# Indexed filling of free page rows and a reordered start, in a fused attention and mixture-of-experts kernel

## The chip, the cores and the metric

The kernel runs on one core of a Trainium2 chip. The metric is device time in microseconds (us) of one execution. The core has a matrix engine (TensorE, PE), a vector engine (VectorE, DVE), a scalar engine (ScalarE, ACT), a general engine (GpSimd, POOL) and SyncE (SP), which here only issues transfers. Each engine works through its own list of instructions in order and waits on semaphores for the others. Transfers run on 16 shared DMA engines.

## The reference

Block-causal attention over 8 batches of 8 heads, 576 tokens and width 64, followed by a mixture of 8 experts in which each of the 4608 tokens goes to its best expert:

```python
scores = scale * np.matmul(q, k.transpose(0, 1, 3, 2))
mask = block_i >= block_j            # blocks of 64
attn = softmax(np.where(mask, scores, -1e9))
x = (attn @ v) -> (4608, 512)        # all heads of a token side by side

logits = x @ w_gate
expert_idx = np.argmax(logits, axis=1)
gate_w = softmax(logits)[arange(N), expert_idx]
for e in range(8):
    rows = tokens with expert_idx == e
    y[rows] = np.maximum(x[rows] @ w1[e], 0) @ w2[e]
return gate_w[:, None] * y
```

## The kernel before

**Two stages.** The attention stage handles 32 head pairs (`PAIRS`), four to a batch. The expert stage handles pages of 128 token rows, each page belonging to one expert. Between them lies `xsorted`, a buffer in device memory with 43 pages (`NP` = 36 + 7). A row has 258 words (`ROW`): 512 half-precision values of x, the gate weight, and the number of the token.

**A head pair.** `load` (L171) fetches q and k of a pair from SP's queue, `load_v` (L185) its v. `cast` (L195) turns q and k to half precision on POOL: two instructions on L199 and one for the tail of 64 tokens on L201. `trans` (L204) transposes them on PE and copies the result out on DVE (L215, L217). `scores` (L225) multiplies, takes the exponential on ACT (L245) and zeroes masked corners on POOL (L247). `sums` (L249) adds tiles on DVE for the denominators; `attend` (L258) multiplies by v (L273); `denominators` (L279) uses the constant `picks`; `finish` (L301) multiplies by `wgi`, which holds an identity and the gate weights side by side (L320), and by `sel` (L316), and divides on DVE. The tiles for q and k and for v have two buffers each, so the load of a pair three ahead waits for a cast, and that of v for an attend.

**A batch.** After its fourth pair `choose` picks each token's expert. Four or five pairs later `route` (L384 to L436) counts tokens by expert and gives each token a slot in `xsorted`; `cnt`, `pages`, `lastA` and `used` carry the state: tokens and pages of each expert so far, where its last page lies, and pages in use. `scatter` (L442) then writes rows to their slots with an indexed DMA from POOL, five to a batch. `load_weights` (L138, L142) fetches the experts' weights in 16 parts of 1 MB, also from POOL's queue.

**Fills.** A page that ends up partly used would hold old data in its free rows. So `fill_pages` (L122) writes rows whose token number is `NO_TOKEN` over pages before tokens arrive: in pairs 0 to 3, eight DMAs from SP cover all 43 pages. Later the rows with `NO_TOKEN` are dropped on output, since the indexed store checks its bounds.

**An expert page.** `step(T)` issues, for PE: the first matmul of page T (`m1`, L626), the transposes of page T+1 (`mtx`, L611), the transposes of the hidden layer of page T-1 (`mth`, L638) and the second matmul of page T-2 (`m2`, L648). ACT computes h of page T (L631) and then y of page T-2 (L651), in this order. POOL stores y by token number (L652). There are two h tiles and two y tiles. `mload` (L602) loads a page five steps ahead from SP; ten page tiles exist. In step 1 the last batch is routed and scattered. `closed`, `first_places` and `orders` pick ten pages that no later token can touch (`FIRST`), so these can start early; their loads do not wait for the last batch's rows.

**Branches.** 36 pages are always processed. Behind them, nested branches on `used` process up to 38, up to 40, or all 43; `ends` holds these counts. 38 pages are processed with the data of the runs shown: the store L652 stands 38 times in the profile.

**Order.** PE, ACT and POOL follow the order written in the main loop during attention (`manual_schedule`, L523); in the expert stage only PE and ACT do (L699). DVE and SP throughout, and POOL in the expert stage, are ordered by the scheduler.

**Start.** Before the first load is used, L51 to L119 and L159 to L167 set up all constants on POOL: identities, triangles, `picks`, `wgi`, `sel`, counters, the `fill` row and borders of tiles.

Of the kernel before, what the change touches and what calls it, by code (L numbers as in the profile page):

```python
# [8 lines left out]
F32 = mybir.dt.float32  # L9
F16 = mybir.dt.float16  # L10
I32 = mybir.dt.int32
# [11 lines left out]
def kernel(  # L23
# [28 lines left out]
    make_identity(nc, ident32)  # L52
    ident16 = consts.tile([128, 128], F16)
    nc.gpsimd.tensor_copy(ident16, ident32)
    before32 = consts.tile([128, 128], F32)
    make_upper_triangular(nc, before32, 1.0, diag=False)
    before16 = consts.tile([128, 128], F16)
    nc.gpsimd.tensor_copy(before16, before32)
    ones16 = consts.tile([128, 128], F16)
    nc.gpsimd.memset(ones16, 1.0)  # L60

    picks = consts.tile([128, 5, 32], F32)
    nc.gpsimd.memset(picks, 0.0)
    for i in range(5):
        nc.gpsimd.memset(picks[:, i, i:i + 1], 1.0)

    wgi = consts.tile([128, HP, 144], F32)
    nc.gpsimd.memset(wgi, 0.0)
    for hp in range(HP):
        nc.gpsimd.tensor_copy(wgi[:, hp, 0:128], ident32)  # L70
        for h in range(2):
            nc.sync.dma_start(
                out=wgi[h * 64:h * 64 + 64, hp, 128 + h * E:128 + h * E + E],
                in_=moe_w_gate[hp * 128 + h * 64:hp * 128 + h * 64 + 64, :])

    GROUP = (0, 1, 0, 1, 0)
    sel = consts.tile([128, 5, 2], F32)
    for i in range(5):
        for h in range(2):
            r = 32 * (2 * h + GROUP[i]) + i  # L80
            nc.gpsimd.tensor_copy(sel[:, i, h:h + 1], ident32[:, r:r + 1])
    ione = consts.tile([128, E], F32)
    nc.gpsimd.memset(ione, 1.0)
    pref_i = consts.tile([128, 5, E], I32)
    nc.gpsimd.iota(pref_i, pattern=[[0, 5], [-1, E]], base=E, channel_multiplier=0)
    pref = consts.tile([128, 5, E], F32)
    nc.gpsimd.tensor_copy(pref, pref_i)
    page_i = consts.tile([128, 1], I32)
    nc.gpsimd.iota(page_i, pattern=[[0, 1]], base=0, channel_multiplier=1)
    page_f = consts.tile([128, 1], F32)  # L90
    nc.gpsimd.tensor_copy(page_f, page_i)
    em_all = consts.tile([128, B], F32)

    FIRST = 10
    order1 = consts.tile([1, 2 * FIRST], I32)
    order2 = consts.tile([1, 2 * (NP - FIRST)], I32)
    place_i = consts.tile([128, NP], I32)
    nc.gpsimd.iota(place_i, pattern=[[1, NP]], base=0, channel_multiplier=0)
    place = consts.tile([128, NP], F32)
    nc.gpsimd.tensor_copy(place, place_i)  # L100
    page_h = consts.tile([128, 1], F16)
    nc.gpsimd.tensor_copy(page_h, page_f)
    nc.gpsimd.memset(em_all, 0.0)
    used_i = consts.tile([1, 1], I32)
    cnt = consts.tile([128, E], F32)
    pages = consts.tile([128, E], F32)
    lastA = consts.tile([128, E], F32)
    used = consts.tile([128, 1], F32)
    for t in (cnt, pages, lastA, used):
        nc.gpsimd.memset(t, 0.0)  # L110


    wall = wpool.tile([128, E, 16, 512], F16)


    fill = consts.tile([128, ROW], I32)
    nc.gpsimd.memset(fill, 0)
    nc.gpsimd.iota(fill[:, 257:258], pattern=[[0, 1]], base=NO_TOKEN,
                   channel_multiplier=0)  # L119
    xs_pages = xsorted.rearrange("(t p) r -> p t r", p=128)  # L120

    def fill_pages(b):  # L122

        def upto(n):
            return min(NP, -(-n * S // 128) + E - 1) if n else 0
        lo, hi = upto(b), upto(b + 1)
        if hi > lo:
            nc.sync.dma_start(out=xs_pages[:, lo:hi, :],
                              in_=fill.unsqueeze(1).to_broadcast([128, hi - lo, ROW]))

    def apart(key, ins):
        tc.declare_no_dep(ins.ins, group=key, reason="scatters to different rows")
# [13 lines left out]
    with tc.tile_pool(name="ld", bufs=2) as ld, \  # L146
# [9 lines left out]
        ptp = probs.enter_context(tc.tile_pool(name="ptp", bufs=2))  # L156

        oTs = [op.tile([128, 640], F32, name=f"oT{i}") for i in range(2)]
        for t in oTs:  # L159
            nc.gpsimd.memset(t[:, 576:640], 0.0)  # L160
        dens = [op.tile([128, 128], F32, name=f"den{i}") for i in range(2)]

        acc = op.tile([128, 2, 512], F32)
        nc.gpsimd.memset(acc[:, :, 448:512], 1.0)
        ohs = [op.tile([128, 5, E], F16, name=f"oh{i}") for i in range(2)]
        for t in ohs:
            nc.gpsimd.memset(t, 0.0)  # L167

        st, yps = {}, []

        def load(p):  # L171
            b, h0 = p // HP, 2 * (p % HP)

            qk = ld.tile([128, 2, 2, 256], F32, name="qk32")
            tl = ld.tile([64, 2, 2, 64], F32, name="tl32")
            for n, src in ((0, q), (1, k)):
                nc.sync.dma_start(
                    out=qk[:, n],
                    in_=src[b, h0:h0 + 2, 0:512, :].rearrange("h (p c) d -> p h (c d)", c=4))
                nc.sync.dma_start(  # L180
                    out=tl[:, n],
                    in_=src[b, h0:h0 + 2, 512:576, :].rearrange("h p d -> p h d"))
            st["qk", p] = (qk, tl)
# [11 lines left out]
        def cast(p):  # L195
            qk, tl = st.pop(("qk", p))
            h16 = op.tile([128, 2, 5, 2, 64], F16, name="qk16")
            for n in range(2):
                nc.gpsimd.tensor_copy(h16[:, n, 0:4].rearrange("p c h d -> p h c d"),  # L199
                                      qk[:, n].rearrange("p h (c d) -> p h c d", c=4))  # L200
            nc.gpsimd.tensor_copy(h16[0:64, :, 4], tl)  # L201
            st["qk16", p] = h16
# [143 lines left out]
        def small(name, w=E):  # L346
            return rp.tile([128, w], F32, name=name)
# [90 lines left out]
        def scatter(b, j):  # L438
# [8 lines left out]
            if b == B - 1:  # L447
                tc.add_to_no_dep_group("last rows", ins.ins)

        def closed():  # L450

            cur, hit = small("cur"), small("hit")
# [56 lines left out]
        def last_experts():  # L509
            st["em_h"] = experts()  # L510
# [12 lines left out]
        with tc.manual_schedule(engines={ET.PE, ET.Activation, ET.Pool}):  # L523
# [9 lines left out]
            for n in range(2):  # L533
                trans(1, n)
            load(2)
            for p in range(PAIRS):
                nxt, more = p + 1 < PAIRS, p + 2 < PAIRS
                if nxt:
                    load_v(p + 1)
                if p + 3 < PAIRS:  # L540
                    load(p + 3)
                for b in ((0,), (1, 2), (3, 4), (5, 6, 7), ())[min(p, 4)]:
                    fill_pages(b)
                if more:
                    cast(p + 2)
                sums(p)
                if nxt:
                    scores(p + 1, 0)
# [106 lines left out]
                in_=y, in_offset=None, bounds_check=N - 1, oob_is_err=False)  # L655
            apart("tokens", ins)

        ends = list(range(-(-N // 128), NP, 2))[:3] + [NP]

        def step(T, n):  # L660
            if T < n:
                m1(T)
            if T == 1:
                route(B - 1)
                for j in range(5):
                    scatter(B - 1, j)
                last_experts()
            if T == 3:
                last_order()
            if T + 5 < ends[0]:  # L670
                mload(T + 5)
            if T == ends[0] - 2:
                for t in range(ends[0], NP):
                    mload(t)
            if T + 1 < n:
                mtx(T + 1)
            if 0 <= T - 1 < n:
                mth(T - 1)
            if 0 <= T - 2 < n:
                m2(T - 2)  # L680
# [58 lines left out]
```

## Time and profile before

| | us |
|---|---|
| median of 3 runs | 470.23 |
| lowest, highest | 461.27, 476.65 |
| the profiled execution | 470.48 |
| its span, first to last instruction | 468.7 |
| its mean granted PE clock | 0.97 |

The page gives, for each engine, the time in which it was busy and its number of instructions; then groups of instructions by line, with the number, the busy time, the mean of one in ns, and behind the second bar the time that the engine stood idle just before them and what ended it. A waiting time `3.73 <-DMA v<-in_v_dram` in a timeline row means that the engine stood idle so long until that transfer had landed. SPq and POOLq rows are the issuing of transfers. The attention stage lies between about 8 and 286 us, the expert stage after it. The transfers that the change touches stand on the page as follows (KB each, and the median us from issue to landing where it is known):

```
xsorted<-x,slot POOLq DMA_INDIRECT x40, 4.1
out_dram<-y,xs POOLq DMA_INDIRECT x38, 2.7
xsorted<-fill SPq DMA_DIRECT2D x4, 516.0 KB
xsorted<-fill SPq DMA_DIRECT2D x3, 645.0 KB
xsorted<-fill SPq DMA_DIRECT2D x1, 1548.0 KB
```

The transfers that fetch q and k are of 256 KB each and 32 KB for the tails; those of v are of 128 and 16 KB, two of each to a pair; a part of the weights has 1024 KB at its destination.

### The profile page before, as it was taken

The numbers are of one execution on the slowest core, as the hardware profiler recorded it, in microseconds if no ns is written. First come the engines' busy times: TensorE is split into PE (matmuls) and PEld (weight loads), VectorE is DVE, ScalarE is ACT, GpSimd is POOL, SyncE is SP. The second block draws the span as 40 slices with busy tenths as digits, with TensorE's granted clock in tenths as the row PEclk, the third lists the DMA queues.
The fourth block names the chain that finished last, engine by engine and source line by source line (L and its number), as shares of the span: only waits on it lengthen the run. The fifth ranks groups of instructions, "written<-read, shape, count | busy, mean of one in ns | idle before, by whom it ended". The sixth has DMA issues, their size and how long they took to land.

```text
span 468.7 us, 11177 instructions
## 1 busy us (share of the span) xinstructions
PE 420.8 (90%) x3870; PEld 260.5 (56%) x3870; DVE 252.2 (54%) x755; ACT 196.6 (42%) x309; POOL 191.3 (41%) x378
## 2 busy tenths in 40 slices
PE   2899879897999999999988897999999999999880
PEld 1466656575666666566656574555555555555430
DVE  2476946894696987977875954422222222222210
ACT  1455435444445454555453431334344343443420
POOL 8263335556347566566274440241222212222120
PEclk9999989999999999999999988899999999999986
DMA  5599979878869988989788478032222223222211
GB/s 138 141 278 242 233 192 230 194 194 200 164 180 208 219 202 187 212 210 190 190 201 206 89 151 197 24 125 96 101 93 85 86 91 103 102 88 75 92 49 43
DMA packets 85195, 71.46 MB, mean 152 GB/s; under 512 B 52240, under 2 KB 79632, under 8 KB 83088
## 3 DMA queue, kind: packets, MB, share of 16 engines
q1 hardware_dynamic: 78000, 39.71, 32.6%
q0 software_dynamic: 7136, 30.98, 27.7%
q8 instruction: 36, 0.59, 0.6%
q14 instruction: 23, 0.19, 0.1%
HBM read 67.56 MB, written 20.40 MB: 188 GB/s over the span
## 4 chain that ended last, share of the span: by engine, by line
issue 24%; DMA 11%; POOL 7%; PE 6%; DVE 4%; SPq 2%; POOLq 1%; DVEq 0%
POOL out_dram L652 7%; DMA v<-in_v_dram 5%; DMA out_dram<-y,xs 5%; PE o L273 3%; DMA xs<-xsorted 2%; PE tp L320 1%; PE tp L296 1%; POOL xsorted L442 1%; DVE qkT L215 1%; SPq L602 1%; DVE acc L251 1%; PE s L242 1%; SPq L192 0%; POOLq L652 0%; DVE acc L253 0%
## 5 line engine op out<-in xcount | busy, mean ns | idle before, releaser
L245 ACT ACTIVATE pt<-s 128x1024 f32<-128x1024 f32 x96 | 94.7, 1022 | 84.9 <-PE s L242 68.0
L273 PE MATMUL o<-pt,v 128*64 128x320 f32 (+3 forms) x768 | 97.1, 397 | 8.1 <-DMA v<-in_v_dram 8.1
L652 POOL DMA_INDIRECT out_dram<-y,xs x38 | 37.4, 984 | 114.2 <-ACT y L651 113.6
L626 PE MATMUL s<-wall,xsT 128*128 x304 | 75.7, 394 | 6.4 <-issue 3.1
L273 PEld LDWEIGHTS o<-pt,v 128*64 128x64 f32 x768 | 56.5, 142 | 44.1 <-issue 12.4
L215 DVE COPY qkT<-tp 128x512 f16<-128x512 f16 x64 | 43.7, 683 | 52.1 <-PE tp L213 52.1
L648 PE MATMUL tp<-wall,hT 128*128 x304 | 71.7, 379 | 0.0
L614 DVE COPY xsT<-o 128x512 f16<-128x512 f16 x38 | 16.1, 424 | 100.5 <-PE o L611 100.5
L247 POOL MEMSET pt<- 64x128 f32 x128 | 23.2, 200 | 97.5 <-ACT pt L245 86.4
L631 ACT ACTIVATE h<-s 128x1024 f16<-128x1024 f32 x38 | 38.9, 1023 | 53.7 <-PE s L626 53.7
L442 POOL DMA_INDIRECT xsorted<-x,slot x40 | 47.4, 1185 | 32.7 <-DVE em_h L471 20.1
L199 POOL CAST qk<-qk 128x512 f16<-128x512 f32 x64 | 50.9, 818 | 19.3 <-DMA qk<-in_q_dram 9.7
L320 PE MATMUL tp<-wgi,oT 128*128 128x144 f32 x320 | 56.0, 309 | 0.0
L626 PEld LDWEIGHTS <-xsT 128*128 128x128 f16 x304 | 30.4, 100 | 44.0 <-issue 7.9
L651 ACT ACTIVATE y<-tp,xs 128x512 f32<-128x512 f32 x38 | 26.1, 687 | 53.7 <-PE tp L648 50.9
L277 ACT COPY oT<-o 128x256 f32<-128x256 f32 x64 | 25.7, 402 | 50.0 <-PE o L273 50.0
L320 PEld LDWEIGHTS tp<-wgi,oT 128*128 128x128 f32 x320 | 43.7, 194 | 3.0 <-issue 0.2
L648 PEld LDWEIGHTS <-hT 128*128 128x128 f16 x304 | 28.4, 98 | 27.2
L251 DVE TENSOR_TENSOR acc<-pt 128x896 f32<-128x896 f32 x32 | 36.3, 1135 | 13.1 <-issue 7.6
L242 PE MATMUL s<-qkT 64*128 64x512 f16 (+4 forms) x320 | 33.7, 302 | 2.5 <-DVE qkT L215 1.8
L211 PE MATMUL tp<-ident,qk 128*128 128x128 f16 x256 | 26.3, 227 | 7.8 <-POOL qk L199 7.8
L641 DVE COPY hT<-o 128x1024 f16<-128x1024 f16 x38 | 26.3, 691 | 12.2 <-PE o L638 9.7
(137 smaller groups left out, 481.9 us busy)
## 6 DMA issues: line engine op xcount, KB each, us to landing
wall<-in_moe_w_dram POOLq DMA_DIRECT2D x16, 1024.0 KB, 9.4
qk<-in_q_dram SPq DMA_DIRECT2D x32, 256.0 KB
qk<-in_k_dram SPq DMA_DIRECT2D x32, 256.0 KB
v<-in_v_dram SPq DMA_DIRECT2D x64, 128.0 KB
xs<-xsorted SPq DMA_DIRECT2D x43, 129.0 KB
xsorted<-fill SPq DMA_DIRECT2D x4, 516.0 KB
xsorted<-fill SPq DMA_DIRECT2D x3, 645.0 KB
xsorted<-fill SPq DMA_DIRECT2D x1, 1548.0 KB
```

The lines of the kernel that those rows point to most:

```text
L199: nc.gpsimd.tensor_copy(h16[:, n, 0:4].rearrange("p c h d -> p h c d"), qk[:, n].rearrange("p h (c d) -> p h c d", c=4))
L215: nc.vector.tensor_copy(qkT[:, n, 0:512].rearrange("d (p c) -> d p c", c=4), ps[:, 0:512].rearrange("d (c p) -> d p c", c=4))
L242: nc.tensor.matmul(out=sp[:, h, o:o + w], lhsT=qkT[r, 1, c * 128:c * 128 + 128], rhs=qkT[r, 0, q0:q0 + w], start=True, stop=True)
L245: nc.scalar.activation(pt[:, :, t * 512:t * 512 + 512], sp, AF.Exp, scale=scale)
L251: nc.vector.tensor_tensor(out=acc[:, :, 0:448], in0=pt[:, :, 128:576], in1=pt[:, :, 576:1024], op=ALU.add)
L273: nc.tensor.matmul(out=o[h * 64:h * 64 + 64, q0 - lo:hi - lo], lhsT=vt[r, c, h, :], rhs=src, start=(c == 0), stop=(c == last), skip_group_ ...
L320: nc.tensor.matmul(out=ps[:, m * 144:m * 144 + 144], lhsT=oT[:, i * 128:i * 128 + 128], rhs=wgi[:, hp, :], start=True, stop=True, skip_gro ...
L442: ins = nc.gpsimd.indirect_dma_start(out=xsorted[:, :], out_offset=bass.IndirectOffsetOnAxis(ap=slot[0:m, j:j + 1], axis=0), in_=x16[0:m, ...
L626: nc.tensor.matmul(out=hp[:, half * 512:half * 512 + 512], lhsT=xT[:, c * 128:c * 128 + 128], rhs=weight(T, 2 * c + half), start=(c == 0), ...
L631: nc.scalar.activation(h, hp, AF.Relu)
L648: nc.tensor.matmul(out=yp, lhsT=hT[:, f * 128:f * 128 + 128], rhs=weight(T, 8 + f), start=(f == 0), stop=(f == 7))
L652: ins = nc.gpsimd.indirect_dma_start(out=out[:, :], out_offset=bass.IndirectOffsetOnAxis(ap=xs[:, 257:258], axis=0), in_=y, in_offset=None ...
```

## The change

Five things are edited.

1. The fills of pairs 0 to 3 go. One fill of the pages from 36 on stays, placed at pair 4 in the loop. The other free rows are computed once the last batch is routed (`free_rows`, six small DVE instructions) and written by eight indexed DMAs from POOL, one for each expert, two in each of the steps 2 to 5 (`fill_rows`). An index that is not a free row is out of bounds and is dropped.
2. k of pairs 0 and 1 is loaded from ACT's queue instead of SP's.
3. k of pairs 0 and 1 is cast on DVE instead of POOL.
4. Constants are set up later: some after the first scores (`borders`, `constants`, then the loads in `gate_weights`), those that only routing uses in pair 1 (`route_constants`). Only the identity stays ahead of the first cast.
5. `ends` has one more level: 36, 38, 40, 42, 43 instead of 36, 38, 40, 43.

```diff
+    row_m = consts.tile([128, 1], F32)
+    row_n = consts.tile([128, 1], F32)
...
+    def gate_weights():
+        for hp in range(HP):
+            for h in range(2):
+                nc.sync.dma_start(
+                    out=wgi[h * 64:h * 64 + 64, hp, 128 + h * E:128 + h * E + E],
+                    in_=moe_w_gate[hp * 128 + h * 64:hp * 128 + h * 64 + 64, :])
+
+    def constants():
+        nc.gpsimd.memset(fill, 0)
+        nc.gpsimd.iota(fill[:, 257:258], pattern=[[0, 1]], base=NO_TOKEN,
+                       channel_multiplier=0)
+
+        nc.gpsimd.memset(picks, 0.0)
...
+        nc.gpsimd.memset(wgi, 0.0)
+        for hp in range(HP):
+            nc.gpsimd.tensor_copy(wgi[:, hp, 0:128], ident32)
...
+    def route_constants():
+        make_upper_triangular(nc, before32, 1.0, diag=False)
...
+        nc.gpsimd.tensor_scalar(row_m, page_f, -128.0, None, op0=ALU.add)
+        nc.gpsimd.tensor_scalar(row_n, page_f, -float(NO_TOKEN), None, op0=ALU.add)
...
+        def borders():
+            nc.gpsimd.memset(acc[:, :, 448:512], 1.0)
+            for t in oTs:
+                nc.gpsimd.memset(t[:, 576:640], 0.0)
+            for t in ohs:
+                nc.gpsimd.memset(t, 0.0)
...
             for n, src in ((0, q), (1, k)):
-                nc.sync.dma_start(
+                eng = nc.scalar if n and p < 2 else nc.sync
+                eng.dma_start(
...
             for n in range(2):
-                nc.gpsimd.tensor_copy(h16[:, n, 0:4].rearrange("p c h d -> p h c d"),
+                eng = nc.vector if n and p < 2 else nc.gpsimd
+                eng.tensor_copy(h16[:, n, 0:4].rearrange("p c h d -> p h c d"),
...
+        def free_rows():
+
+            got, w = small("got"), small("frw")
+            nc.vector.scalar_tensor_tensor(out=got, in0=pages, scalar=-128.0, in1=cnt,
+                                           op0=ALU.mult, op1=ALU.add)
+            nc.vector.tensor_scalar(got, got, row_m, None, op0=ALU.is_le)
+            nc.vector.scalar_tensor_tensor(out=w, in0=lastA, scalar=-1.0, in1=pages,
+                                           op0=ALU.add, op1=ALU.add)
+            nc.vector.tensor_scalar(w, w, 128.0, row_n, op0=ALU.mult, op1=ALU.add)
+            nc.vector.tensor_tensor(out=w, in0=w, in1=got, op=ALU.mult)
+            rows = rp.tile([128, E], I32, name="frows")
+            nc.vector.tensor_scalar(rows, w, float(NO_TOKEN), None, op0=ALU.add)
+            st["free"] = rows
+
+        def fill_pages():
+
+            nc.sync.dma_start(out=xs_pages[:, N // 128:, :],
+                              in_=fill.unsqueeze(1).to_broadcast([128, NP - N // 128, ROW]))
+
+        def fill_rows(n):
+            ins = nc.gpsimd.indirect_dma_start(
+                out=xsorted[:, :],
+                out_offset=bass.IndirectOffsetOnAxis(ap=st["free"][:, n:n + 1], axis=0),
+                in_=fill, in_offset=None, bounds_check=NP * 128 - 1, oob_is_err=False)
+            apart("rows", ins)
+            tc.add_to_no_dep_group("last rows", ins.ins)
...
             load(2)
+            borders()
+            constants()
+            gate_weights()
             for p in range(PAIRS):
...
-                for b in ((0,), (1, 2), (3, 4), (5, 6, 7), ())[min(p, 4)]:
-                    fill_pages(b)
                 if more:
                     cast(p + 2)
+                if p == 1:
+                    route_constants()
+                if p == 4:
+                    fill_pages()
...
-        ends = list(range(-(-N // 128), NP, 2))[:3] + [NP]
+        ends = list(range(-(-N // 128), NP, 2)) + [NP]
...
                 for j in range(5):
                     scatter(B - 1, j)
+                free_rows()
                 last_experts()
+            if 2 <= T < 6:
+                for e in range((T - 2) * E // 4, (T - 1) * E // 4):
+                    fill_rows(e)
```

## The prediction

> **What bounds the kernel now.** I read the page first (busy shares, costliest groups), then the waits of TensorE (PE), then the timeline at the places where it waits.
>
> ```profile
> PE 420.8 (90%) x3870; PEld 260.5 (56%) x3870; DVE 252.2 (54%) x755; ACT 196.6 (42%) x309; POOL 191.3 (41%) x378
> L273 PE MATMUL o<-pt,v 128*64 128x320 f32 (+3 forms) x768 | 97.1, 397 | 8.1 <-DMA v<-in_v_dram 8.1
> ```
>
> PE is the bound in both stages, so a change is worth what it does to PE's gaps. The row L316 comes once a head pair; its starts are 7.71 us apart where nothing waits (24.66, 32.37, 40.08, 47.80) and 8.62 where a batch is routed. In the expert stage the page rhythm is 4.18 us. Three places matter here. The start:
>
> ```profile
> 7.14 1.16 POOL L199 CAST qk<-qk 128x512 f16<-128x512 f32 x2
> 7.79 0.61 PE L211 MATMUL tp<-ident,qk 128*128 128x128 f16 x4 [7.79 <-POOL qk L199]
> 10.41 1.03 PE L242 MATMUL s<-qkT 64*128 64x512 f16 x6 [0.79 <-DVE qkT L215]
> ```
>
> POOL is busy without a break from 0.75 to 7.14 us with constants, and only then casts q and k one after the other; PE waits 7.79 us for it. Next, 56 to 70 us:
>
> ```profile
> 46.94 3.10 SPq L128 DMA_DIRECT2D xsorted<-fill  x3
> 50.15 1.33 SPq L189 DMA_DIRECT2D v<-in_v_dram  x1
> 54.60 3.60 SPq L192 DMA_DIRECT2D v<-in_v_dram  x1
> 57.47 0.61 PE L242 MATMUL s<-qkT 64*128 64x512 f16 x6
> 61.81 4.48 PE L273 MATMUL o<-pt,v 128*64 128x256 f32 x24 [3.73 <-DMA v<-in_v_dram]
> 60.00:68.00 8.00, 6.05 (x48) 4.20 (x49) 1.80 (x8) 1.06 (x3) 2.95 (x6) 0.79 0.63 166
> ```
>
> Three fills (13 pages of 129 KB, 1.68 MB) are issued just ahead of v; issuing itself slows to 3.60 us for one load; the DMA engines are full (share 1.05 in 52 to 60 us); PE waits 3.73 us for v. The 24 matmuls that follow take 4.48 us against 2.81 us elsewhere, and the granted clock of that window is 0.79 (the column after POOL). The interval of L316 is 13.37 us (56.42 to 69.79): 5.65 above 7.72. Two later v waits, of 2.2 and 2.1 us, have no fill near them (intervals of 12.19 and 10.45 us, together 7.2 above rhythm). Last, the early expert stage:
>
> ```profile
> 306.41 0.90 POOL L442 DMA_INDIRECT xsorted<-x,slot  x1 [0.30 <-issue]
> 307.62 1.00 POOL L652 DMA_INDIRECT out_dram<-y,xs  x1 [0.30 <-issue]
> 308.92 0.99 POOL L652 DMA_INDIRECT out_dram<-y,xs  x1 [0.30 <-issue]
> 314.70 0.69 ACT L651 ACTIVATE y<-tp,xs 128x512 f32<-128x512 f32 x1 [1.42 <-PE tp L648]
> 316.43 1.02 ACT L631 ACTIVATE h<-s 128x1024 f16<-128x1024 f32 x1 [1.05 <-PE s L626]
> 320.57 0.66 PE L638 MATMUL o<-ident,h 128*128 128x128 f16 x8
> ```
>
> Five scatters of the last batch go out from 301.34 at about 1.27 us each; the first output rows, ready at 302.56, already wait for them until 307.62. After two outputs POOL has caught up.
>
> [...] a wait of 3.73 us was followed by 1.67 us of slowness, one of 2.2 us by about 2.3, so I add 1.9 us to each wait of that size. [...] The trace cannot show two issuing queues; it shows 229, 190 and 165 GB/s in the third, fourth and fifth microsecond. [...]
>
> **Part by part.** In the order of the built program:
>
> *First loads and casts.* k of pairs 0 and 1 is issued by ACT and cast by DVE; POOL makes only the identity (0.75 to 1.4 us) before its cast of q. The bytes decide: 576 KB (q, k and their tails of pair 0) had moved by about 4.9 us (23, 229, 190 and most of 165 KB in microseconds 1 to 5). With two queues interleaved, q and k come together at about 4.5 to 4.9, plus an estimated 0.7 until the semaphore is seen, judged from the 1.1 us between the first issue (0.76) and the first bytes (1.9). Cast of q 0.62, identity to f16 0.28: first transposes at 6.3 (5.7 to 6.9) instead of 7.79. The tail's cast (0.39) follows, while DVE has cast k beside it; before, k's cast and the tail put the second transposes at 8.85, now about 7.0. So scores start 1.9 us earlier; I take **2.0** (1 to 3[...]). ACT's four issues (about 0.6 each) and its table load (1.28) end at 4.6, before its first exponential. VectorE's room instruction, once first in its queue, moves behind pair 1.
>
> *Constants moved.* After pair 0's four memsets, which end at 14.33 us in the trace and so at about 12.3 then, POOL does borders, fill, picks, the gate tile and sel: 0.19+0.22+0.19+0.42+0.45+1.54+1.24 = 4.3 us, to about 16.6; the cast of pair 2 (1.8 us) ends at 18.4, and its transposes (21.54 in the trace) are due at 19.5. Hidden with 1 us to spare. The eight gate loads sit behind four pairs' loads and the one remaining fill in SP's queue, and wait for the gate memset: issued about 14 to 19 us (8 x 0.6), landed by 21; their first reader L320 is due at about 22. Zero, at most 1.5. The second group of constants (about 20 small instructions, 3.0 us by their rows) follows pair 3's cast at about 24 us and holds the memsets of pair 2, which are not needed before 31, and VectorE's room, queued ahead of pair 3's transposes' copies, due at 27.5. Zero, at most 1.
>
> *Fills dropped.* Eight fills of 43 pages, 5.68 MB, become one of 7 pages, 0.92 MB, which stands early in SP's queue, before the gate loads. 4.76 MB leave the queue. Up to 48 us PE waited for none of it: no gain. At 50 to 62 us v no longer has 1.68 MB ahead of it: **-5.6**. The floor is 0, if the weight load issued at 47.31 on POOL's queue holds v back instead; the ceiling is -12.8, if the two later v waits (7.2) go too, which no fill explains. SP's order of v against q also shifts by a few places later on; its price is unknown, I take 0 (-3 to +3).
>
> *Fills by index.* Six VectorE instructions of 128x8 (0.15 us each) at page 1 delay the next page's copy by 0.6 us; PE is in 1.89 us of matmuls then. Zero. Eight indirect DMAs, priced as the indexed stores they resemble (0.98 + 0.30 = 1.28 us), come on POOL's queue in this order: five scatters, two fills, output 0, six fills, output 1, output 2. Output 0 goes from 307.62 to 310.2; output 1 from 308.92 to 301.34 + 5 x 1.26 + 9 x 1.28 = 319.2. There are two y tiles, so y of page 3 (due 314.70) waits until output 1 has landed: 319.2 + 2.7 (median of the DMA issues) = 321.9. Behind it on ACT is h of page 6 (due 316.43): it ends at 321.9 + 0.7 + 1.0 = 323.6, and PE's transposes of h, due 320.57, wait **3.0 us**; with 1.9 of half clock **+4.9**. If most indices, being out of range, make a fill cost half (0.64), output 1 is 5.1 earlier and nothing waits: floor 0. If the landing counts from the end of POOL's work and a fill takes 1.5, the wait is 6: ceiling +8. Page 10's load now waits for the last fill too (about 321); it is read at about 332: zero.
>
> *The extra branch level.* Both programs leave at 38 pages by the same branches: zero.
>
> Sum: -2.0 - 5.6 + 4.9 = **-2.7 us** against the profiled execution's 470.5 (its span 468.7 and 1.8 around it), which stands 0.25 above the median of 470.23: 467.5, rounded to **467**.
>
> **The rivals.** *A, POOL's jam costs nothing*: for it, POOL is 0.13 to 0.24 busy later in the stage and the fills mostly skip rows; against it, output 0 already waited 5 us behind five scatters. 463 us. *B, the later v waits go as well* (DMA share falls, loads gain a lead): for it, the runs of before spread by 15 us, as such waits would; against, loads are held to two buffers, so no lead survives 60 us. 467 - 7 = 460. *C, slower*: the v wait at 58 us belongs to the 1 MB weight load and not to the fills; it would stay, leaving -2.0 + 4.9 = +2.9, so 473. It decides if v of pair 5 lands after 58.1 us (its attend's turn), less the 2 us of the earlier start. For it: the two later waits stand beside weight loads alone; against: other pairs with a weight load run at 7.71. To be slower by over 2% (9.4 us) it would need a jam at its ceiling (+8) too and a little more. That the fills are not dropped is excluded: the built queue of SP has one.
>
> **How the numbers follow.** Likeliest case 0.47, A 0.15, B 0.18, C 0.15, C with the long jam 0.05. A change of 2% is about what a measurement of this kernel can tell from none. Faster by that (below 461) takes B and half of what A and B share: 0.20. Slower by it (above 480) takes the last case and some of C's upper end: 0.08. The rest, 0.72, is within 2%. The range, from B's 460 less its spread to C's 473 plus the spread of the runs shown, is 458 to 475.
>
> **What would show it.** First L211 on PE near 6.3 us and first L242 near 8.5. No PE wait for v between 50 and 70 us, an L316 interval of 7.7 to 8.6 there, DMA share below 0.9. POOL rows of two fills, one output, six fills; then one ACT wait for an output of about 7 us, PE's L638 late by about 3 us and half clock after it. The forecast is wrong if v still waits at 56 us, if fills take under 0.9 us each, or if L320 or the copies of pair 3 wait for constants.

## The result, and the profile after

The changed kernel takes **475.81 us** (median of 4 runs, 474.19 to 478.99), the kernel before 465.75 us (4 runs, 461.04 to 476.65): a ratio of **1.033, 95% interval 1.022 to 1.043**. It is slower, and outside the range of 458 to 475. (Two of the four runs of the kernel before, and its profiled execution, were slow runs; medians here are of all runs, ratios of the fast ones alone, which makes the ratio larger than the 1.022 of the medians.) The profiled execution took 474.19 us, its span is 472.4 us.

Line numbers have moved: L276 is the old L273 (attention), L661 the old L626 (first expert product), L673 the old L638 (transposes of h), L683 the old L648 (second product), L687 the old L652 (output). L473 is the indexed fill.

From the page: busy shares, and two of the costliest groups.

```profile
PE 417.0 (88%) x3870; PEld 256.9 (54%) x3870; DVE 253.9 (54%) x763; ACT 196.3 (42%) x309; POOL 201.9 (43%) x386
...
L661 PE MATMUL s<-wall,xsT 128*128 x304 | 76.7, 398 | 20.2 <-DVE xsT L649 12.0
L276 PE MATMUL o<-pt,v 128*64 128x320 f32 (+3 forms) x768 | 93.0, 389 | 0.6 <-DMA v<-in_v_dram 0.6
```

The columns of the groups are number, busy time, mean of one in ns, and idle time just before them with what ended it. The 8.1 us of waits for v have gone to 0.6. In their place the first expert product waits 20.2 us. The start, from the timeline of the changed kernel:

```profile
4.64 0.54 DVE L202 CAST qk<-qk 128x512 f16<-128x512 f32 x1 [4.64 <-DMA qk<-in_k_dram]
4.85 0.48 POOL L54 CAST ident<-ident 128x128 f16<-128x128 f32 x1
...
5.39 0.59 PE L214 MATMUL tp<-ident,qk 128*128 128x128 f16 x4 [5.39 <-POOL ident L54]
...
7.63 1.03 PE L245 MATMUL s<-qkT 64*128 64x512 f16 x6 [0.79 <-DVE qkT L218]
```

The first scores come at 7.63 us, not 10.41. The stretch in which v was late, by windows of 8 us (the columns are PE, PEld, DVE, ACT, POOL, granted clock, DMA share, GB/s):

```profile
52.00:60.00 8.00, 7.49 (x90) 5.13 (x90) 7.78 (x38) 3.75 (x8) 4.17 (x9) 1.00 0.75 197
60.00:68.00 8.00, 7.85 (x93) 5.13 (x88) 5.45 (x14) 4.04 (x8) 5.41 (x11) 1.00 0.69 129
```

TensorE is busy 7.85 of 8 us where it was busy 6.05, at a granted clock of 1.00 where it had 0.79. The loss comes 220 us later, while GpSimd issues its row of indexed transfers. For comparison, the first product of two pages in a row in the kernel before, 4.18 us apart:

```profile
310.27 1.89 PE L626 MATMUL s<-wall,xsT 128*128 x8
...
314.45 1.89 PE L626 MATMUL s<-wall,xsT 128*128 x8
```

From the timeline of the changed kernel:

```profile
287.96 0.66 PE L673 MATMUL o<-ident,h 128*128 128x128 f16 x8
...
288.45 1.89 PE L683 MATMUL tp<-wall,hT 128*128 x8
...
290.18 1.89 PE L661 MATMUL s<-wall,xsT 128*128 x8
...
291.48 1.00 POOL L473 DMA_INDIRECT xsorted<-fill,frows  x1 [0.30 <-issue]
...
293.09 0.69 DVE L676 COPY hT<-o 128x1024 f16<-128x1024 f16 x1 [4.51 <-PE o L646]
...
299.53 0.69 ACT L686 ACTIVATE y<-tp,xs 128x512 f32<-128x512 f32 x1 [10.77 <-remote]
...
303.11 0.98 POOL L687 DMA_INDIRECT out_dram<-y,xs  x1 [0.30 <-issue]
...
306.67 0.42 DVE L649 COPY xsT<-o 128x512 f16<-128x512 f16 x1 [12.88 <-remote]
306.67 1.02 ACT L666 ACTIVATE h<-s 128x1024 f16<-128x1024 f32 x1 [6.45 <-remote]
...
307.24 3.57 PE L661 MATMUL s<-wall,xsT 128*128 x8 [11.02 <-DVE xsT L649]
```

The copy of hT (293.09) waits for TensorE and nothing else. The transposes that it reads ended at 288.6 by the trace; it starts at 293.09. Then y starts 9 us after its product, and h and xsT at 306.67. Between the first matmuls of two pages lie **17.06 us instead of 4.18** and then, at half clock (granted clock 0.50, 8 matmuls in 3.57 us instead of 1.89), 6.14. That is 14.8 us lost in one place. The end, where the program chooses how many pages to run, in the kernel before and in the changed one:

```profile
447.11 3.57 PE L626 MATMUL s<-wall,xsT 128*128 x8 [3.06 <-issue]
```

```profile
441.12 1.89 PE L683 MATMUL tp<-wall,hT 128*128 x8
...
448.86 3.57 PE L661 MATMUL s<-wall,xsT 128*128 x8 [5.86 <-issue]
```

TensorE's wait at the branch, 3.06 us before, is 5.86 us. The trace names nothing that it waits for ("issue").

### The profile page after: what moved, and what is told of

Its sections match the earlier page's. It is cut to its first block, busy times and chain, and to the rows that moved or that the text cites. A ratio compares the mean times of both kernels' runs of the same rounds, so it can differ in the third digit from the quotient of the medians.

```text
span 472.4 us, 11203 instructions
## 1 busy us (share of the span) xinstructions
PE 417.0 (88%) x3870; PEld 256.9 (54%) x3870; DVE 253.9 (54%) x763; ACT 196.3 (42%) x309; POOL 201.9 (43%) x386
## 4 chain that ended last, share of the span: by engine, by line
issue 24%; POOL 8%; PE 6%; DMA 6%; DVE 5%; POOLq 1%; ACT 0%; DVEq 0%; ACTq 0%
POOL out_dram L687 6%; DMA out_dram<-y,xs 6%; PE o L276 2%; POOL xsorted L473 1%; PE tp L323 1%; PE s L661 1%; PE tp L299 1%; DVE acc L254 1%; DVE qkT L218 1%; POOL xsorted L445 1%; DVE acc L256 1%; DVE x L336 1%; DMA xsorted<-fill,frows 1%; POOLq L687 0%; ACT pt L248 0%
## 5 line engine op out<-in xcount | busy, mean ns | idle before, releaser
L661 PE MATMUL s<-wall,xsT 128*128 x304 | 76.7, 398 | 20.2 <-DVE xsT L649 12.0
L276 PE MATMUL o<-pt,v 128*64 128x320 f32 (+3 forms) x768 | 93.0, 389 | 0.6 <-DMA v<-in_v_dram 0.6
L687 POOL DMA_INDIRECT out_dram<-y,xs x38 | 37.4, 983 | 122.9 <-ACT y L686 122.3
L276 PEld LDWEIGHTS o<-pt,v 128*64 128x64 f32 x768 | 53.5, 139 | 35.9 <-issue 7.4
L683 PE MATMUL tp<-wall,hT 128*128 x304 | 72.4, 382 | 0.0
L661 PEld LDWEIGHTS <-xsT 128*128 128x128 f16 x304 | 30.6, 101 | 58.8 <-DVE xsT L649 14.0
L323 PE MATMUL tp<-wgi,oT 128*128 128x144 f32 x320 | 55.0, 305 | 0.0
L202 POOL CAST qk<-qk 128x512 f16<-128x512 f32 x62 | 49.3, 819 | 11.9 <-DMA qk<-in_k_dram 5.9
L683 PEld LDWEIGHTS <-hT 128*128 128x128 f16 x304 | 28.6, 99 | 27.7 <-issue 1.1
```

The costliest lines, as they stand in the source:

```text
L202: eng.tensor_copy(h16[:, n, 0:4].rearrange("p c h d -> p h c d"), qk[:, n].rearrange("p h (c d) -> p h c d", c=4))
L276: nc.tensor.matmul(out=o[h * 64:h * 64 + 64, q0 - lo:hi - lo], lhsT=vt[r, c, h, :], rhs=src, start=(c == 0), stop=(c == last), skip_group_ ...
L323: nc.tensor.matmul(out=ps[:, m * 144:m * 144 + 144], lhsT=oT[:, i * 128:i * 128 + 128], rhs=wgi[:, hp, :], start=True, stop=True, skip_gro ...
L661: nc.tensor.matmul(out=hp[:, half * 512:half * 512 + 512], lhsT=xT[:, c * 128:c * 128 + 128], rhs=weight(T, 2 * c + half), start=(c == 0), ...
L683: nc.tensor.matmul(out=yp, lhsT=hT[:, f * 128:f * 128 + 128], rhs=weight(T, 8 + f), start=(f == 0), stop=(f == 7))
L687: ins = nc.gpsimd.indirect_dma_start(out=out[:, :], out_offset=bass.IndirectOffsetOnAxis(ap=xs[:, 257:258], axis=0), in_=y, in_offset=None ...
```

## Experiments

The columns of the table: the old fills at pairs 0 to 3, the list of page counts at which the program may end ("changed" is 36, 38, 40, 42, 43, "old" 36, 38, 40, 43), the indexed transfers in a row without a pause on GpSimd in the early expert stage, the longest interval between the first matmuls of two pages from the first of these transfers on, TensorE's wait at the branch (these three from the profiled execution), and the time.

| kernel | old fills | list | in a row | longest | branch | median us | ratio to before |
|---|---|---|---|---|---|---|---|
| before | yes | old | 7 | 4.4 | 3.1 | 465.8 | |
| changed | no | changed | 15 | 17.1 | 5.9 | 475.8 | 1.022 to 1.043 |
| old fills back | yes | changed | 6 | 4.6 | 6.6 | 468.8 | 1.008 to 1.016 |
| old levels | no | old | 15 | 17.0 | 3.5 | 472.6 | 1.008 to 1.026 |
| eight empty fills | yes | changed | 15 | 17.0 | 4.6 | 484.0 | 1.034 to 1.053 |
| spare pages | no | changed | 15 | 17.1 | 5.8 | 476.7 | 1.019 to 1.041 |
| four empty fills | yes | changed | 10 | 10.1 | 4.6 | 475.1 | 1.019 to 1.040 |
| spread fills | no | old | 8 | 7.2 | 2.4 | 457.4 | 0.983 to 0.992 |
| start only | yes | old | 6 | 4.6 | 1.7 | 462.8 | 0.988 to 0.996 |
| early numbers | no | changed | 17 | 5.9 | 4.9 | 462.2 | 0.996 to 1.004 |
| later fills | no | old | 7 | 4.4 | 2.0, 2.6 | 456.1 | 0.983 to 0.991 |
| plain writes, early | yes | changed | 7 | 4.4 | 4.6 | 467.0 | 1.009 to 1.017 |
| plain writes, in place | yes | changed | 5 | 5.2 | 5.2 | 470.9 | 1.009 to 1.021 |
| two more levels | yes | 36, 38, 40, 41, 42, 43 | 7 | 4.4 | 1.9 | 461.5 | 0.991 to 0.999 |
| other four levels | yes | 36, 38, 42, 43 | 6 | 4.6 | 1.8 | 461.3 | 0.980 to 0.994 |

Each ratio is an interval at 95%, against runs of the kernel before on the same chip (medians 463.1 to 467.0). The sets of runs differ in chip and in that median, so small differences between rows are better read from the ratios. A row of transfers counts indexed scatters, fills and outputs until the first pause above 0.5 us; the expectations say fourteen where output 1 makes it fifteen.

**Which part costs.** The old fills put back, all else as changed:

```diff
-                if p == 4:
-                    fill_pages()
+                for b in ((0,), (1, 2), (3, 4), (5, 6, 7), ())[min(p, 4)]:
+                    fill_pages(b)
...
-                free_rows()
...
-            if 2 <= T < 6:
-                for e in range((T - 2) * E // 4, (T - 1) * E // 4):
-                    fill_rows(e)
```

> The changed kernel with the old page fills at pairs 0 to 3 in place of the one fill and the eight indexed fills; the new start, the moved constants and the extra branch level stay. Theory 1 (the eight indexed fills cost about 14 us in the early expert stage, most of the loss): the stretch from the last L316-like copy of the attention stage to page 6's first matmul falls from 42.9 us to 29 (27 to 31), and the time falls from 475 to about 462 (459 to 466). Theory 2 (the fills by index cost only the predicted 5, the rest is something else in the new order of queues or the branch level): the stretch stays above 37 us and the time above 467. If v waits again behind the old fills, one interval between 56 and 70 us is about 13 us instead of 7.7; both theories allow that.

The interval fell from 17.06 to 4.63 us and the time to 468.8: the indexed fills bring the stall. The time stayed above the 466 that theory 1 allowed, since v waits again behind the fills (one interval of 13.0 us between two head pairs) and the branch still costs. The same kernel with the eight indexed fills added, every index out of range, so that they write nothing:

```diff
-            nc.vector.tensor_scalar(rows, w, float(NO_TOKEN), None, op0=ALU.add)
+            nc.vector.tensor_scalar(rows, w, 0.0, float(NO_TOKEN), op0=ALU.mult, op1=ALU.add)
```

> The kernel with the old page fills (first of this group) plus the eight indexed fills of the change at their place, with every index set out of range: 8 indexed transfers that write nothing. Theory A (rows out of range hold up the engines): at least as bad as the changed kernel, the stretch to page 6's first matmul 43 to 46 us, 14 us or more above the first of this group. Theory B (any indexed transfer in a row does it, by GpSimd's 1.28 us each): stretch 41 to 44 us. Theory C (the written bytes do it): stretch 29 to 31 us, as without the fills, time within 2 us of the first of this group.

484.0 us, **15.2 more** than without them, interval 17.01. The bytes are no part of it. In this run TensorE's own matmuls come apart. From its timeline:

```profile
300.88 1.24 PE L687 MATMUL tp<-wall,hT 128*128 x5
...
302.45 0.59 PE L687 MATMUL tp<-wall,hT 128*128 x2 [0.33 <-issue]
...
304.58 0.38 PE L687 MATMUL tp<-wall,hT 128*128 x1 [1.54 <-issue]
...
306.75 0.69 ACT L690 ACTIVATE y<-tp,xs 128x512 f32<-128x512 f32 x1 [10.73 <-remote]
```

Eight matmuls of one product, with all operands at hand, take 4.1 us with gaps that no other engine explains. So here it is TensorE itself that does not go on, and not only the copies that are late. Instruction fetches are not the reason: in the changed kernel none is in the trace between 283.3 and 311.1 us, and TensorE goes on at 307.1.

**What it is about the fills.** Not the rows out of range: here each fill writes all 128 rows, the unneeded ones to a spare page of its own.

```diff
-                in_=fill, in_offset=None, bounds_check=NP * 128 - 1, oob_is_err=False)
+                in_=fill, in_offset=None)
```

(beside it, `xsorted` is E pages longer, and the row list sends other rows to page NP + n; with one spare page for all eight there is no measured time)

> The changed kernel, but each indexed fill sends the rows that are not free to its own spare page instead of out of range, with no bounds given: all 128 rows of each of the eight are written. The run with empty fills has shown that the bytes of the fill are not needed for the stall; open is whether the dropped rows are. Theory A (rows dropped as out of range hold up the engines): the 17 us between the first matmuls of two pages in the early expert stage goes to 4.2 to 6, the time from 475 to 459 to 464. Theory B (the number of indexed transfers in a row on GpSimd's queue does it, whatever they write): the 17 us stay, within 2, and the time is 473 to 478. Mixed: 8 to 13 us.

The interval is 17.07 us, the time 476.7: theory B. Then four empty fills instead of eight, one for a page step (`fill_rows(T - 2)` for T of 2 to 5):

> The kernel with the old fills and empty indexed fills, but four of them, one for a page step, in place of eight, two for a step. If the cost goes by the count of transfers, the interval of 17 us falls to about 10 to 12 and the time from 484 to 475 to 478. If there is a threshold (the crowding of two and more for a page step), the interval falls to below 6 and the time to 468 to 471, as without any empty fill.

The interval is 10.07 us, between the 4.63 of no empty fill and the 17.01 of eight: it goes by the count. The median is 475.1.

Plain writes instead of indexed ones, first with a source that is ready early, then with one that is ready only when the row list is:

```diff
-            ins = nc.gpsimd.indirect_dma_start(
-                out=xsorted[:, :],
...
+            nc.gpsimd.dma_start(out=spare[n * 128:(n + 1) * 128, :], in_=st["free"])
```

> The kernel with the old fills and, at the place of the eight indexed fills, eight plain (not indexed) writes of one page each to spare pages, issued on the same GpSimd queue, two for a page step. If the crowd on GpSimd's queue is enough, whatever the kind: an interval of 12 to 17 us as with the indexed ones, time 480 to 485. If it takes indexed transfers, whose addresses are made from a list: the longest interval is about 4.6 us and the time 469 to 471.

This one told nothing: with no late operand the writes were issued at 12.7 to 21.3 us, where they held up the gate weights by 3 us (467.0 us).

> The run with plain writes failed to put them in the row: they were issued at 12.7 to 21.3 us. Here the eight plain writes carry the row list itself, which is ready only after the last batch is routed, so they stand where the change has its indexed fills (two, output 0, six, output 1). Everything else as with the empty indexed fills (484.0 us, interval 17.0). If any crowd on GpSimd's queue holds up TensorE's register reads: an interval of 9 to 17 us and 476 to 485 us. If it takes indexed transfers: no interval above 6 us and 468 to 471 us.

In place, the eight plain writes leave intervals of 4.44, 5.20 and 4.17 us; 470.9 us, close to the 468.8 of the kernel without any. They are shorter on GpSimd (six in 3.22 us, where an indexed one takes 1.29 with its gap), but plain and indexed ones together keep GpSimd busy without a pause for 14.3 us, from 294.15 to 308.48, and the row of ten indexed ones that gave 10.07 lasted 12.5. So in these runs it took indexed transfers, not a busy queue.

**What of TensorE it holds.** Once a page, between the transposes of x and those of h, TensorE reads the page's expert number from SBUF into a register (`number`, called in `mtx`). The timeline leaves these reads out; the view of their source line, in the changed kernel, has them:

```profile
L630 PEldq TENSOR_LOAD <-order x38: 297/300/487, 273.3 to 438.2; - x38
```

(The three numbers are the shortest, the median and the longest in ns.) None is recorded as long, and the one in the stall, at 289.8 us, takes 0.30 us. But TensorE's next address computation for L661, which uses the number read there, is recorded only at 307.1; in the page before, 2.0 us lie between the two. Here all reads of the first ten pages are made before the first step:

```diff
-            pg["e", T] = number(T, 1, ET.PE, E - 1)
+            if T >= FIRST:
+                pg["e", T] = number(T, 1, ET.PE, E - 1)
...
+            for T in range(FIRST):
+                pg["e", T] = number(T, 1, ET.PE, E - 1)
             mtx(0)
```

> The changed kernel, but TensorE reads the expert numbers of the first ten pages into its registers before the first page step instead of one in each step. In the stall, copies that wait for TensorE alone start 4.5 to 13 us after its matmuls ended in the records, and TensorE's own matmuls stop with nothing named that they wait for. Theory R (the register read, which TensorE makes once per page between the transposes, is what hangs while GpSimd issues indexed transfers back to back): the interval of 17 us between first matmuls falls to 4.2 to 5, and the time from 475 to 459 to 463. Theory S (TensorE's work or signals themselves are held, whatever it reads): the interval stays at 15 to 17 us and the time within 3 us of 475.

This is what theory R said. The row is as in the changed kernel, but that the last fill comes after output 1 and two more outputs join it, and the time is **462.2 us instead of 475.8** (1.000 of the kernel before instead of 1.033). So, by this one build in 20 runs, the 17 us interval is gone once the reads are out of the page loop (5.92). That the read itself hangs is not shown, since its record is short: the signals of TensorE's work that come late may be what is held behind it. From the timeline of this run, the end of the row:

```profile
298.72 1.89 PE L662 MATMUL s<-wall,xsT 128*128 x8
...
302.04 0.98 POOL L688 DMA_INDIRECT out_dram<-y,xs  x1 [0.30 <-issue]
...
302.90 1.89 PE L662 MATMUL s<-wall,xsT 128*128 x8
...
304.62 0.98 POOL L688 DMA_INDIRECT out_dram<-y,xs  x1 [0.30 <-issue]
...
304.90 0.69 ACT L687 ACTIVATE y<-tp,xs 128x512 f32<-128x512 f32 x1 [5.41 <-PE s L662]
...
305.48 1.02 ACT L667 ACTIVATE h<-s 128x1024 f16<-128x1024 f32 x1
...
306.55 0.71 PE L674 MATMUL o<-ident,h 128*128 128x128 f16 x8 [1.54 <-ACT h L667]
...
307.10 1.89 PE L684 MATMUL tp<-wall,hT 128*128 x8
...
307.50 0.69 ACT L687 ACTIVATE y<-tp,xs 128x512 f32<-128x512 f32 x1 [1.00 <-DMA out_dram<-y,xs]
...
308.82 1.89 PE L662 MATMUL s<-wall,xsT 128*128 x8
```

Pages run at 4.18 us through the whole row, and only then comes the chain that the prediction described: output 1 goes out at 302.04, y of page 3 starts 2.86 us later, at 304.90, h follows it, and L638 (here L674) is 1.54 us late. The releaser named for y is TensorE, whose product was long done. For the next y, at 307.50, the trace names the landing of an output, which was issued 2.88 us before, at 304.62; the 2.86 us agree with that. One interval is 5.92: 1.74 us in all.

**A version without the stall.** Spread over page steps, with twenty places instead of ten taken from pages closed before the last batch, so that loads need not wait; old list of page counts:

```diff
-    FIRST = 10
+    FIRST = 20
...
-            if 2 <= T < 6:
-                for e in range((T - 2) * E // 4, (T - 1) * E // 4):
-                    fill_rows(e)
+            if 4 <= T < 4 + E:
+                fill_rows(T - 4)
```

> The changed kernel with the old list of page counts for the end, the eight fills one for a page step from page 4 to page 11, and the page loads that wait for them from page 20 on instead of page 10 (the first 20 places in the order instead of 10 are taken from pages closed before the last batch). If crowding sets the stall: no page interval above 6 us in the early stage, time 472.6 of the kernel with old levels less about 13 = 457 to 461, below the kernel before. If each indexed fill costs a fixed 1.8 us wherever it stands: several page intervals of 5 to 6.5, time 469 to 474.

> The spread fills two page steps later (pages 6 to 13), so that no fill stands between the five scatters and the first outputs. The row of indexed transfers without a pause falls from eight to six. If the stall goes by the length of that row (7.2 us interval at eight, 4.6 at six, 10.1 at ten, 17.1 at fourteen): the interval falls from 7.2 to about 4.6 and the time from 457.4 to 454 to 456. If any fill within the first pages costs the same wherever it stands: 457 to 459.

> The same kernel as the run with the fills at pages 6 to 13, measured over more rounds, since four runs gave no interval: it is the version that should be below both kernels. From its sum (462.8 of the start alone, less 5 to 8 for the dropped fills, no stall) 455 to 458, 0.975 to 0.99 of the kernel before; if the four runs were a lucky set, 459 to 463 and a ratio that takes in 1.

From page 4 on: 457.4 us, longest interval 7.2. From page 6 on: every interval from the first scatter on at 4.2 to 4.4, 456.6 us (4 runs) and **456.1 us in 22 runs, ratio 0.987 (0.983 to 0.991)**. It is below both kernels. The last shift took away the 3 us of the longest interval, but no gain in time is shown for it: the ratios are 0.988 (0.983 to 0.992) and 0.987.

**The start and the branch.** The first part of the change alone (old fills, old list, no indexed fills):

> The kernel before with the first part of the change alone: loads on two queues, constants later; old fills, no indexed fills, old page counts for the end. The prediction's step of 2.0 us (measured in the changed kernel's trace: 2.7 at the first copy of attention) should be all that is left: 463 to 465 against 466.5 before; and the branch's interval should be 7 to 8 us, not 9 to 11. If it is 467 or more, the moved constants or the new order of queues cost something that the prediction put at zero.

462.8 us, and the first matmul with `sel` (L316, one per head pair) at 22.98 us (24.66 before). The old list alone put back in the changed kernel, and two other lists on the kernel with the start alone:

```diff
-        ends = list(range(-(-N // 128), NP, 2)) + [NP]
+        ends = list(range(-(-N // 128), NP, 2))[:3] + [NP]
```

> The changed kernel with the old list of page counts at which the program may end (three and the last) instead of one for every second page. Theory 1 (the extra levels cost something where the branch is taken): the 5.9 us wait of TensorE at the branch falls to about 3.1 us as before, and the end after it by up to 1 us: time 471 to 473 instead of 475. Theory 2 (the predicted zero: the wait is longer for another reason, as the fills' late landing): the wait stays at 5 to 6 us and the time within 1 us of 475.

> The kernel with the start changes alone, with two more page counts for the end (36, 38, 40, 41, 42, 43 instead of 36, 38, 40, 43). All leave at 38. If every level adds instructions that TensorE must fetch before it goes on: the branch interval (6.0 us without, 10.9 with one more level) goes to 10 to 15 us, with at least three instruction fetches in it against two, and the time from 462.8 to 467 to 473. If the level count doesn't matter and the interval only varies from build to build: 6 to 8 us and 461 to 465.

> The kernel with the start changes alone, with four page counts for the end as before, but 36, 38, 42, 43 in place of 36, 38, 40, 43. The list of the change (36, 38, 40, 42, 43) has shown waits of 4.6 to 6.6 us at the branch in seven builds; the old list 1.7 to 3.5 in five and one with 36, 38, 40, 41, 42, 43 1.9. If the wait goes with the length of code that is jumped over in one piece, this list (four pages between 38 and 42) gives 4 to 7 us, and 465 to 468 us in all; if it takes the nesting of exactly five levels, 1.7 to 3.5 us and 461 to 465.

With the old list: 472.6 instead of 475.8, wait 3.5 instead of 5.9 us. The list costs something, then, in the changed kernel and, as "old fills back" against "start only" shows, with the old fills too (468.8 and 462.8, wait 6.6 and 1.7). But two more levels gave 1.9 us of wait and 461.5 us, and 36, 38, 42, 43 gave 1.8 us and 461.3: neither the number of levels nor the length of code between two of them makes it, and both my accounts fell. What the traces do show is instruction fetches, on queue q8. From the DMA view of the changed kernel, 444.0 to 448.8 us:

```profile
q8 instruction: 1, 0.02, 1.3%
```

and of the kernel with two more levels, 433.0 to 438.9 us, the whole wait:

```profile
q8 instruction: 1, 0.02, 1.7%
```

(The columns are packets, MB, and share of the DMA engines' time.) In the second, one fetch of 16 KB on q8, begun at 435.5 to 435.9 us, is all; TensorE goes on at 438.94. In the first, two fetches begun at 441 and 442 us come before this one, which begins at 446.3 to 446.6, 4.2 us after the second; TensorE goes on at 448.86. All eight builds with the changed list have such a late fetch (3.1 to 4.6 us after the one before) and waits of 4.6 to 6.6 us; of eight executions with other lists, four have a single fetch and four a pair 0.9 to 1.2 us apart, with waits of 1.7 to 3.5. So the longer wait goes with the late fetch; that the fetch is its cause is not shown, and why this list and no other has it stays open.

## Why the prediction was wrong

**First loads and casts (-2.0): right, and larger.** First transposes at 5.39 (6.3 was said), first scores at 7.63 (8.5), the first L316 2.73 us earlier in the changed kernel. The kernel with the start alone is 3.6 us below the 466.4 of its group, but its trace has only 1.7 of that at the first L316; another 1.4 is a shorter wait at the branch. The casts of q and k began at 4.29 and 4.64, not at the 5.2 to 5.6 that the arrival (4.5 to 4.9) and 0.7 for the semaphore make: the queues moved 326 GB/s in the fourth microsecond, where I had reckoned with the 190 of the kernel before. Beside VectorE's casts of k, GpSimd's cast of the identity took 0.48 us (0.28 in the kernel before) and its cast of q of pair 1 0.84 (0.60 to 0.61 there), about 0.2 us more each.

**Constants moved (0): in its bounds of 1, but not nothing.** TensorE waits for no gate tile. The second group does come out late, as the bound said; the copies of pair 3 wait for it, which the prediction had named as a sign of being wrong. From the changed kernel's timeline:

```profile
27.70 0.17 DVE L415 SCALAR_TENSOR_TENSOR room<-pages,cnt 128x8 f32<-128x8 f32 x1 [2.30 <-POOL pages L123]
27.78 0.68 DVE L218 COPY qkT<-tp 128x512 f16<-128x512 f16 x1
...
28.71 0.27 PE L299 MATMUL tp<-pt,picks 128*32 128x128 f32 x1 [0.82 <-DVE qkT L220]
```

VectorE's room stands ahead of the copies of pair 3 and waits for the last memsets. The first interval of attention is 8.39 us instead of 7.71: +0.7, out of the start's gain.

**Fills dropped (-5.6): right, size near.** The interval of 13.37 us is 7.71 in the changed kernel and 7.7 in all six further executions without the old fills; of the eight more with them it is 12.0 to 14.9 in six and 9.3 to 9.5 in two. By medians, the run with empty fills and the changed kernel, which differ in the old fills and in what the indexed ones write, stand 8.2 us apart (5 by their ratios to the kernel before). Rival C is excluded: the weight load is still there and nothing waits. Rival B's two later waits for v, 4.3 us in all, are 0.6 here, but no gain can be credited for it: in the other executions such waits come to 0 to 2.9 us, with the old fills and without. That the time came out near C's 473 is chance.

**Fills by index (+4.9): the step that failed.** Its count was right: order, 1.29 us each, output 1 at 17.92 us after the first scatter (17.9 was worked out). Its mechanism exists, as the run with early numbers shows, at 1.74 us instead of 4.9: there one fill fell behind output 1, which went out 16.6 us after the first scatter, 1.3 us sooner; y started 2.86 us after its issue, near the 2.7 that I took, so the wait is 1.54 us at L638 and not 3.0, and no half clock followed (the next product, L684, took 1.89 us for its eight matmuls). But the stall that decides, 14.8 us in the trace and 15.2 by medians, is another, which the prediction does not have: during a row of fifteen indexed transfers on GpSimd, TensorE, which reads a register in each page, does not go on (17.06 us between the first matmuls of two pages; 5.92 with the reads made before). I listed the queues that the fills stand in and the engines that wait for their results; I did not list what TensorE itself reads from SBUF outside its matmuls. Nor did the kernel before give it away: with seven in a row there, no page was late.

The matmul rows of the changed kernel hide the stall. By their records the matmuls at 288 to 292 us were done; their readers start 4.5 to 14.6 us after the recorded ends (hT at 293.09, y at 299.53, h at 306.67).

**The extra branch level (0): the second step that failed.** That the same branches are taken is true, and the list cost 3.2 us by medians in the changed kernel and 6.0 between the kernels "old fills back" and "start only". The waits at the branch grew by 2.4 and 4.9 us, most of this by medians, about half by the ratios (9.4 us between the last two). I priced what is executed and left out what the list changes around it; what that is stays open.

The sum with measured terms, by medians, is -3.6 - 8.2 + 15.2 + 3.2 = +6.6; measured is +10.1, or +9.4 against the 466.4 of the experiments. With 6.0 for the branch it is +9.4 too, but that is no check: start only, old fills back, eight empty fills and the changed kernel then form one chain of steps from the kernel before, which closes whatever the steps are. By the ratios these steps are -3.7, +9.4, +14.5 and -5.0, some +15 in all, so their sizes are uncertain by several us. With the two failed terms as predicted, the change would have gained.

## What to carry to other kernels

Here fifteen indexed transfers in a row on GpSimd came with a page interval of 17.1 us instead of 4.2, though TensorE waits for none of them, while it read a register from SBUF in each page. Spread over the loop they left 4.4 (later fills), and with the reads made before the loop the row left 5.9. In a kernel with such a row and such reads, measure both. Of a busy loop, list for each engine the reads that the timeline does not show. And where data decide which branch is taken, measure the program with its list of branches, not only the path that is taken.

## What the runs showed of the hardware that was not expected

- TensorE's longest page interval by indexed transfers in a row, with a register read in each page: 4.4 us at seven (four builds), 7.2 at eight, 10.1 at ten, 17.0 to 17.1 at fifteen (four builds). From seven to fifteen that is 12.6 us, on average 1.6 for each: its own 1.29 and a little more. But the count does not settle whether the stall begins: three builds with six in a row have 4.6, with y 3.6 us late. In every build with a late y, in the rows of six, eight, ten and fifteen, ScalarE's first late instruction after the row starts 1.3 to 2.7 us after the row's last transfer has ended on GpSimd; in the rows of fifteen one y comes out within the row. Why some builds have no stall at seven, and by what path TensorE is held, was not settled.
- An indexed transfer that writes no row cost GpSimd as much as one that writes 128: 0.98 us (eight empty fills) and 0.96 to 0.98 us (the scatters of 128 rows in the changed kernel).
- After the 11.02 us wait in the changed kernel TensorE ran at half clock (granted 0.50 from 307.24 to 310.81 us) for one page, 1.96 us more; after its wait of 1.54 us it did not (granted 1.00 from 293.84 to 296.22). In the kernel before, the wait of 3.73 us for v was followed by 0.50 from 61.81 to 63.50 us.
- At the branch TensorE waited 4.6 to 6.6 us in the eight executions with a late instruction fetch, and 1.7 to 3.5 in the eight without one.
